# Two attention blocks on one core: row sums inverted after one transfer within SBUF, maxima 40 steps ahead instead of 32, operand splitting spread out, a new written order of the main loop

## The chip, the cores and the metric

The kernel runs on one core of a Trainium2 chip. The metric is the device time of that core in microseconds (us), the median of three runs. One further execution was recorded by the profiler; every duration below comes from that one. Engines are named as in its page: PE (TensorE, matmuls) with PEld (its weight loads), DVE (VectorE), ACT (ScalarE), POOL (GpSimd), SP (SyncE, which here only issues DMAs).

## What is computed

The inputs are two independent blocks, A and B, each with x of 1 x 2048 x 640, a wqkv of 640 x 1920 and a wo of 640 x 640, all float32, 32 heads of 20 columns. The outputs are joined on the last axis.

```
qkv = x @ wqkv
# A: each position attends to itself and to 7 earlier ones, 2 apart
idx = pos[:, None] - 2 * arange(8)[None, :]
logits = einsum("bhsd,bhswd->bhsw", q, k[idx]) * 20**-0.5     # masked where idx < 0
a = einsum("bhsw,bhswd->bhsd", softmax(logits), v[idx]) @ wo
# B: full attention over 2048 positions
b = (softmax(q @ k.T * 20**-0.5) @ v) @ wo
out = concatenate([a, b], axis=-1)
```

## The kernel before

**Operands.** Every product that needs more than the multiplier's format is made of three passes over a high and a low part (`PASSES`). A tile is loaded into a staging buffer (`stg`, three of them), cast to the high part (`first` in `parts`, by default ACT), and the low part is the subtraction raw minus high (`second`, by default DVE), L152. `split` (L157) issues the load and calls `parts` a given number of ticks later.

**Stages.** First K and Q of B are projected and stored to DRAM. Then V of B is projected in 16 groups, and between its matmuls stand the first *maxima*. After that comes the main loop of 512 steps (32 units of 4 heads x 512 queries, 16 key blocks each). One step of B is: 4 score tiles of 128 keys x 512 queries (PE), 4 exponentials of them (ACT), and 4 accumulating products with V and a column of ones (PE, `b_pv`, L436), which also gives the row sums. The maximum that is subtracted enters the scores as extra rows of q, so it must be known first: a separate pass makes the scores once more, transposed, and DVE takes their maxima (4 tiles of 128 x 512 per step, `m_reduce`, L343). That pass runs `LEAD` steps ahead: 2 x LEAD pairs of tiles are reduced between V's matmuls (L890 to L903), and as many steps at the end of the loop have no maxima.

**Order.** PE, ACT and DVE follow a written table, `ORDER` (from L946): Y is one score tile and one maxima tile, S two score tiles, M two maxima tiles that DVE reduces in one instruction, F one *token* of a projection group (two half-height matmuls side by side, 30 tokens a group), V the end of a step. The digits are PSUM banks; there are eight, one of them holds the running product with V. F groups work off the projections of A (`a_group`, L712), then A's output projection (`oa_group`) and B's (`ob_group`); groups that are left at the end run whole (`leftover`).

**POOL and SP.** POOL does A's attention (`a_scores`, `a_values`, L475 to L528). How much of it stands in each step is set by a counter that adds an assumed time per instruction (L62) and lets POOL's list run up to `STEP` us per step (L937, L938). SP issues almost every DMA from one queue in program order, so a DMA that waits for its data holds up all that stand behind it. `after(n, ...)` places an action n ticks (steps) later.

**The chain of a unit's sums.** When a unit ends, ACT copies the product out (`misc`), and `normalize` (L413) does the following: four rows of sums go to DRAM (`s_d<-misc`) and back as 128 x 16 (`sm<-s_d`), DVE inverts them, they go to DRAM (`s_d<-sm`) and return spread over the rows (`misc<-s_d`), POOL multiplies (`misc<-misc`), and the result is stored (`ot_b<-misc`). Its ticks are 1, 2, 7, 8, 9, 11 and 12 after the unit.

**The chain of maxima.** After the last tile of a unit `max_rows` (L299) transposes on DVE, casts and subtracts on POOL, and stores four pieces three ticks later (`mdr<-mtr`). They are read into the rows of q (`last<-mdr`, `s_maxima`) 9 ticks after the scores of the unit before have begun.

Of the kernel before, what the change touches and what calls it, by code (L numbers as in the profile page):

```python
# [41 lines left out]
LEAD = 32  # L42
# [3 lines left out]
STEP = 2.8  # L46
# [5 lines left out]
class InOrder:  # L52
# [5 lines left out]
    def __getattr__(self, name):  # L58
        op = getattr(self.engine, name)

        def emit(*a, **k):
            if name.startswith("tensor_"):  # L62
                n = math.prod(a[0].shape[1:])
                self.us += 0.2 + n * (0.00081 if name == "tensor_copy" else 0.0017 if len(a[0].shape) == 4 else 0.00212)
            return self.tc.keep_in_program_order(op(*a, **k))  # L65
        return emit
# [3 lines left out]
def attention_pair(ctx, tc, xa, wqk_a, wv_a, wo_a, xb, wqk_b, wv_b, wo_b, oa, ob):  # L70
# [86 lines left out]
    def split(hi, lo, src, wait, first=None, second=None, tag=("stg", 3)):  # L157
# [5 lines left out]
        sp.dma_start(raw, src)  # L163
        after(wait, parts, hi, lo, raw if len(hi.shape) == len(raw.shape) else t[:, :n], first, second,
              int(tag[0] == "stg"))
# [21 lines left out]
    def wide_pieces(src, W, half, wait, first=None, second=None):  # L187
        def piece(a, b):
# [3 lines left out]
            split(w[0][:, a:b], w[1][:, a:b], src[half][:, a:b], wait, first, second)  # L192
# [106 lines left out]
    def max_rows(u, m4):  # L299
# [14 lines left out]
        after(3, store)  # L314
# [47 lines left out]
    def s_half():  # L362
# [50 lines left out]
    def normalize(raw, u, then):  # L413
# [3 lines left out]
        s_d = dr.tile([2, GH, 512], F32, tag="s_d", bufs=4, name="s_d")  # L417

        def bcast():
            for j in range(GH):  # L420
                sp.dma_start(misc[32 * j:32 * j + 32, 512:], s_d[1, j].partition_broadcast(32))
# [8 lines left out]
        after(t[2], dve.reciprocal, sm, sm)  # L430
        after(t[3], sp.dma_start, s_d[1].rearrange("j (p c) -> j p c", c=16), sm)
        after(t[4], bcast)
        after(t[5], gp.tensor_tensor, raw, raw, misc[:, 512:], ALU.mult)
        after(t[6], then or out)
# [96 lines left out]
    def a_attention():  # L531
# [5 lines left out]
        for n, (t, c) in enumerate(UNITS):  # L537
            while any(a_rows[u[1] >= 4] <= u[0] for u in UNITS[n:n + 3]) or c == 4 and len(done_a) > 1:
                yield False
            a_fetch(n + 2)  # L540
# [4 lines left out]
            if c == 4:  # L545
                run_jobs(soft_jobs, 1)
                for _ in soft.pop(t):
                    run_jobs(soft_jobs, 1)
            if c < 4:
                yield from a_scores(t, c, a_kv.pop(n))  # L550
# [3 lines left out]
            else:  # L554
                yield from a_values(t, c - 4, a_kv.pop(n))
                if c == WIN - 1:
                    done_a.append([1, t, a_t.pop(t)[2]])
# [6 lines left out]
    def a_turn(t, o):  # L564
# [12 lines left out]
        for k in range(KC):  # L577
            job(turn_jobs, 1 + k, part, k)

    def a_back():  # L580
# [76 lines left out]
    def set_pieces(si, wait):  # L657
# [6 lines left out]
        def split_piece(b, raw):  # L664
# [3 lines left out]
            parts(AW[si][0][:, :, c:c + n], AW[si][1][:, :, c:c + n], raw, second=gp if si < 6 else dve, end=1)  # L668
            if b == len(bits) - 1:
                set_in.add(si)  # L670
# [22 lines left out]
    def xa_pieces(n):  # L693
        def piece(k):
# [3 lines left out]
            after(3, split_piece, k, raw)  # L698
# [13 lines left out]
    def a_group(si, n, a, ns):  # L712
        assert si in set_in and n in x_in, (si, n)
        if n % 2 == 0 and a == 0:
            if si + 1 < NA:
                spaced(set_pieces(si + 1, 3), 1, 2)
            else:
                spaced(wide_pieces(wo_a, WO, 0, 3, dve.tensor_copy), 1, 2)
# [15 lines left out]
    def a_done():  # L734
# [3 lines left out]
        spaced(wide_pieces(wo_a, WO, 1, 3, dve.tensor_copy), 1, 2)  # L738
# [3 lines left out]
    def oa_group(p, half, ns):  # L742
        assert ready_a[0] >= 2 * p + 2, (p, ready_a)
# [41 lines left out]
    def ob_group(qc, a, half, ns):  # L785
        assert ob_ready[0] > qc, (qc, ob_ready)
# [131 lines left out]
    def begin(i):  # L918
# [28 lines left out]
        "Y10Y32M5S47S10M2V4Y75Y61S02Y37Y56VS10Y72Y36VY51Y20Y76VY35Y21F07FFFFY36FFY52FFFY13FFY56FFFY21VM5S32VY31Y56V"  # L947
        "Y23Y51FFFFFY62FFY35FFFY16FFY23FFFM5Y21VY03S72M5VY01Y73S25VS60Y17Y32VM5S70S21VM5S37S02VM5S13Y70VY21Y65F37FFFF"
        "Y20FFY16FFFY52FFM0FFFM5VVY20Y51FFFY46FFY02FFY15FFY64FFFY02FFFF16FFY45FY30FFY72FFY54FFY30FFS72FFFM4V3VY07Y24F"
        "FFFFY05FFY72FFFY40FFY57FFFS24VS05Y71Y62VY40Y51Y27VY46Y05Y12VY74Y06Y51VY72Y40Y56VM0Y27Y45VS62M0S47VY65Y42S01V"  # L950
        "S76S54Y20VY71S60VS54M1Y76VY50Y41F27FFFFY65FFY40FFFY16FFM4FFFM0VVY64Y05FFY31FFFY46FFY50FFY13FFFY46FFFF51FFY30"
        "FY42FFY67FFY03FFY24FFFFFM6M2V0VVY64FY27FFFFY36FFY24FFFY37FFY62FFFM3VY67Y52F13FFFFY46FFY75FFFY24FFY76FFFS52V"
        "S47M5FFFFFFY42FFFFY57FY46FFFFY25VY74Y61S35VY27Y46Y13VY52Y47Y16VY35Y24Y17VY63M4S21VY76Y23S14VS57Y62Y31VY45Y27"
        "Y61VY43Y25F76FFFFY14FFY32FFFY15FFFM3FFM1VVY35Y41FFFY20FFY35FFY41FFY20FFFY35FFFY42M0S37Y65V4Y23Y70Y16VS52Y73"
        "Y01VY56Y32Y17VY05S63M1VY07F56FY31FFFY20FFY73FFFY21FFY70FFFM2VY71Y20FFFFY37FFY12FFFY30FFY17FFFM2FVS01M6Y25V"
        "Y30M6S12VY53Y01Y26VY57M0S32VY56Y73S20VS15Y67Y23VY01Y57Y63VY02F15Y76FFFFY03FFY27FFFY60FFM2FFFM6VVY20Y63FFY74F"
        "FY02FFFY63FFY47FFFY02FFFF64FFY37FY10FY52FFFY37FFY01FFY52FFFY73V0VY51Y27FFFFFY35FFY12FFFY37FFY51FFFM2VM6Y15"
        "Y42VS31M6S45VY32Y14Y76VY53F21Y47FFFFY65FFY43FFFY67FFFM3FFM5VVY37Y54FFFFFY63FFY75FFFY64FFY37FFFM5VM3S72Y15V"
# [161 lines left out]
```

## Time and profile before

| what | us |
|---|---|
| median of three runs (lowest, highest) | 1766.27 (1761.41, 1768.66) |
| the profiled execution's own time | 1765.94 |
| its span, first to last instruction | 1764.0 |
| PE, DVE, ACT, POOL busy | 1716.7, 1394.8, 1239.4, 957.2 |
| mean granted clock of PE | 0.989 |

A busy time is the time in which an engine had an instruction under way. PE's matmuls overlap and their ends are modelled, so its 97% doesn't mean that it could take no more. The stages can be told apart by what runs: K and Q of B until 147 us, V of B with the first maxima until 234, the main loop with maxima until 1642, the 32 steps without maxima until 1716, and the end.

### The profile page before, as it was taken

The page shows a single profiled execution, that of the slowest core. Times are in us where ns is not written, and L with a number is a line of the kernel's source. Part 1 is how long each engine was busy: PE and PEld are TensorE (multiplying, and loading weights), DVE is VectorE, ACT ScalarE, POOL GpSimd, SP SyncE. Part 2 cuts the span into 40 slices and gives each one's busy share as a digit, 9 for nine tenths or more (in the row PEclk, how much of TensorE's full clock was granted, in tenths as well). Part 3 has the DMA queues.
Part 4 walks back from the last instruction along what each step waited for, and adds up shares of the span by engine and source line. Part 5 has one row for each costly group of instructions (what it writes and reads, how often), then busy time and mean ns, then how long its engine had stood idle before and what let it go on. Part 6 is the DMA issues. An engine that isn't in the chain of part 4 may idle for free.

```text
span 1764.0 us, 37708 instructions
## 1 busy us (share of the span) xinstructions
PE 1716.7 (97%) x14273; PEld 1028.8 (58%) x14273; DVE 1394.8 (79%) x2083; ACT 1239.4 (70%) x2415; POOL 957.2 (54%) x857
## 2 busy tenths in 40 slices
PE   9999999999999999989999999999999999999999
PEld 7889955656655655545565555435565444443569
DVE  4326988899888888879899989988789999889101
ACT  4221278787788787777877777677777878877981
POOL 0000210100196469898899999799998994011420
PEclk9999999999999999999999999999999999999999
DMA  7675532214453365546665776367765673121222
GB/s 254 217 237 177 167 92 59 72 51 113 143 163 107 97 203 177 157 160 180 192 188 164 202 202 184 117 163 198 189 180 162 179 200 83 47 89 55 77 67 79
DMA packets 206982, 257.70 MB, mean 146 GB/s; under 512 B 98344, under 2 KB 132532, under 8 KB 205808
## 3 DMA queue, kind: packets, MB, share of 16 engines
q1 hardware_dynamic: 206164, 254.55, 49.1%
q8 instruction: 112, 1.84, 0.5%
q10 hardware_dynamic: 636, 0.74, 0.1%
q14 instruction: 70, 0.57, 0.1%
HBM read 190.31 MB, written 64.24 MB: 144 GB/s over the span
## 4 chain that ended last, share of the span: by engine, by line
PE 81%; DVE 9%; DMA 3%; POOL 3%; ACT 2%; issue 2%; SPq 1%; DVEq 0%; POOLq 0%; ACTq 0%
PE ps_st L65 81%; DVE mx L65 7%; DVE w L65 2%; POOL akv L65 2%; ACT big L65 1%; ACT last L65 1%; SPq L65 1%; DMA s_d<-sm 0%; DMA last<-qb_d 0%; POOL ao L65 0%; DMA stg<-xa 0%; DMA last<-xb 0%; DMA stg<-wo_a 0%; DMA ot_b<-misc 0%; POOL misc L65 0%
## 5 line engine op out<-in xcount | busy, mean ns | idle before, releaser
L65 DVE TENSOR_REDUCE mx<-ps_st 128x1 f32<-128x512 f32 (+1 forms) x1750 | 1255.1, 773 | 144.3 <-PE ps_st L65 136.3
L65 ACT ACTIVATE big<-ps_st 128x512 f32<-128x512 f32 x1172 | 636.4, 619 | 162.5 <-PE ps_st L65 149.2
L65 PE MATMUL ps_st<-big,last 60*128 60x512 f32 x2048 | 694.6, 434 | 10.9 <-DVE mx L65 9.9
L65 PE MATMUL ps_st<-last,big 62*128 62x512 f32 x2048 | 671.8, 427 | 28.3 <-DVE mx L65 15.5
L65 ACT ACTIVATE last<-ps_st 128x512 f32<-128x512 f32 x876 | 475.1, 619 | 117.6 <-PE ps_st L65 108.4
L65 PEld LDWEIGHTS ps_st<-last,big 62*128 62x128 f32 x2048 | 315.8, 186 | 396.1 <-DVE mx L65 121.9
L65 PE MATMUL ps_st<-w,big 64*128 64x320 f32 (+1 forms) x4560 | 491.7, 308 | 2.3 <-DVE mx L65 2.3
L65 PEld LDWEIGHTS ps_st<-w,big 64*128 64x128 f32 (+1 forms) x4560 | 432.4, 187 | 33.0 <-DVE mx L65 5.3
L65 PE MATMUL ps_st<-big,vb 128*32 128x512 f32 x2344 | 387.2, 609 | 0.0
L65 PEld LDWEIGHTS ps_st<-big,last 60*128 60x128 f32 x2048 | 311.2, 185 | 96.7 <-DVE mx L65 46.6
L65 PE MATMUL ps_st<-last,vb 128*32 128x512 f32 x1752 | 311.6, 611 | 0.1
L65 POOL TENSOR_TENSOR akv<-akv 128x640 f32<-128x640 f32 (+3 forms) x304 | 283.9, 934 | 21.4
L65 POOL TENSOR_TENSOR akv<-akv,aq 128x1280 f32<-128x1280 f32 x64 | 189.2, 2957 | 18.6 <-DMA akv<-ka_d 18.6
L65 POOL TENSOR_TENSOR akv<-akv,al 128x1280 f32<-128x1280 f32 x64 | 152.1, 2377 | 1.8 <-DMA akv<-va_d 1.7
L65 PEld LDWEIGHTS ps_st<-big,vb 128*32 128x32 f32 x2344 | 62.6, 108 | 101.3 <-issue 96.6
L65 POOL TENSOR_TENSOR misc<-misc 128x512 f32<-128x512 f32 x31 | 39.8, 1284 | 137.0 <-DMA misc<-s_d 68.4
L65 PE MATMUL ps_st<-w,last 64*128 64x320 f32 (+1 forms) x900 | 103.6, 308 | 0.0
L65 POOL CAST mtr<-mxt 128x32 fp32r<-128x32 f32 x32 | 6.7, 210 | 170.5 <-DVE mxt L65 170.5
L65 POOL TENSOR_TENSOR big<-last,big 128x1024 fp32r<-128x1024 f32 x4 | 9.5, 2406 | 155.1 <-ACT big L65 155.1
L65 PEld LDWEIGHTS ps_st<-last,vb 128*32 128x32 f32 x1752 | 48.7, 109 | 73.3 <-issue 69.9
L65 DVE TENSOR_TENSOR last<-ps_st,last 128x512 fp32r<-128x512 f32 x40 | 27.4, 690 | 77.5 <-ACT last L65 75.5
L65 PEld LDWEIGHTS ps_st<-w,last 64*128 64x128 f32 (+1 forms) x900 | 85.9, 187 | 3.5
(69 smaller groups left out, 879.3 us busy)
## 6 DMA issues: line engine op xcount, KB each, us to landing
akv<-ka_d SPq DMA_DIRECT2D x128, 320.0 KB
akv<-va_d SPq DMA_DIRECT2D x128, 320.0 KB
last<-qb_d SPq DMA_DIRECT2D x128, 160.0 KB
kb_d<-last SPq DMA_DIRECT2D x20, 512.0 KB
qb_d<-last SPq DMA_DIRECT2D x20, 512.0 KB
big<-kb_d SPq DMA_DIRECT2D x16, 640.0 KB
last<-qb_d SPq DMA_DIRECT2D x128, 80.0 KB
misc<-s_d SPq DMA_DIRECT2D x124, 64.0 KB
```

What stands on the lines that cost most here:

```text
L65: return self.tc.keep_in_program_order(op(*a, **k))
```

## The change

- `LEAD` is 40: 16 more pairs of maxima stand between V's matmuls (three per half group instead of two in every second group), and 40 steps have none. The store of the maxima is 6 ticks after the unit instead of 3, their load 5 ticks after the scores of the unit before have begun instead of 9.
- `normalize` moves the sums from SBUF to SBUF in one DMA (`sm<-misc`) instead of two through DRAM. Its ticks are 1, 5, 6, 10, 12, 14: POOL's product and the store of it are two ticks apart instead of one.
- New `parts_apart`: the cast on ACT, then the subtraction on DVE in two halves, one and two ticks later. It is used for the weights of A's second half and for wo_a, whose casts were on DVE. wo_b's casts move from DVE to ACT and its subtractions to POOL. Loads of the weights of A's projections and of wo_a are 3 ticks apart instead of 2, and these and xa are given 4 ticks to land instead of 3.
- The casts of A's transposed rows (`a_back`) move from POOL to ACT.
- POOL's list: 0.08 us more is assumed for each instruction, and `STEP` is 2.72 instead of 2.8. The loads for the next piece of A stand behind the first instruction of a piece instead of ahead of it. The transposes of A's rows on DVE come two ticks later.
- `ORDER` is a new table. It holds 2070 F tokens instead of 2100, so one more group runs whole at the end. In the first 128 steps it has 705 F tokens instead of 600.

```diff
-LEAD = 32
+LEAD = 40
-STEP = 2.8
+STEP = 2.72
-                self.us += 0.2 + n * (0.00081 if name == "tensor_copy" else 0.0017 if len(a[0].shape) == 4 else 0.00212)
+                self.us += 0.28 + n * (0.00081 if name == "tensor_copy" else 0.0017 if len(a[0].shape) == 4 else 0.00212)
+    def parts_apart(hi, lo, raw, then=None):
+        act.copy(hi, raw)
+        n = hi.shape[1] if len(hi.shape) == 3 else 1
+        step = -(-n // 2)
+        for d, a in enumerate(range(0, n, step)):
+            b = min(a + step, n)
+            after(1 + d, dve.tensor_tensor, *(t[:, a:b] if n > 1 else t for t in (lo, raw, hi.bitcast(F32))), ALU.subtract)
+
+        def end():
+            live[0] -= 1
+            if then:
+                then()
+        after(2, end)
...
-        after(3, store)
+        after(6, store)
...
-                after(9, s_maxima, u + 1)
+                after(5, s_maxima, u + 1)
...
-        t = (1, 2, 5, 6, 7, 9, 10) if then else (1, 2, 7, 8, 9, 11, 12)
-        after(t[0], sp.dma_start, s_d[0], raw[DH:128:32])
-        after(t[1], sp.dma_start, sm, s_d[0].rearrange("j (p c) -> j p c", c=16))
...
+        t = (1, 4, 5, 8, 10, 11) if then else (1, 5, 6, 10, 12, 14)
+        after(t[0], sp.dma_start, sm, raw[DH:128:32].rearrange("j (p c) -> j p c", c=16))
...
-            a_fetch(n + 2)
...
+            next(work)
+            yield
+            a_fetch(n + 2)
+            yield from work
...
-            job(turn_jobs, 1 + k, part, k)
+            job(turn_jobs, 3 + k, part, k)
...
-            parts(ot[:, 0], ot[:, 1], r, gp.tensor_copy, gp, 1)
+            parts(ot[:, 0], ot[:, 1], r, second=gp, end=1)
...
-            after(3, split_piece, k, raw)
+            after(4, split_piece, k, raw)
...
-                spaced(wide_pieces(wo_a, WO, 0, 3, dve.tensor_copy), 1, 2)
+                spaced(wide_pieces(wo_a, WO, 0, 4, apart=True), 1, 3)
...
-                spaced(wide_pieces(wo_b, WO, 0, 3, dve.tensor_copy) + wide_pieces(wo_b, WO, 1, 3, dve.tensor_copy), 1, 2)
+                spaced(wide_pieces(wo_b, WO, 0, 3, second=gp) + wide_pieces(wo_b, WO, 1, 3, second=gp), 1, 2)
...
-                    if k in (0, 8):
+                    if k in ((0, 5, 10) if o else (0, 8)):
...
-        "Y10Y32M5S47S10M2V4Y75Y61S02Y37Y56VS10Y72Y36VY51Y20Y76VY35Y21F07FFFFY36FFY52FFFY13FFY56FFFY21VM5S32VY31Y56V"
+        "Y01Y23M4S67S01M2V6Y47Y05S12M3Y07VY51F23Y40FFFFY75FFY14FFFY07FFY15FFFY04VY71Y50FFFFFY47FFY15FFFY40FFY71FFFM4V"
```

Where it moves instructions, at three places. First PE while V of B is projected: two matmuls `ps_st<-big,last` are a pair of maxima tiles, `ps_st<-w,...` are V's half matmuls, 30 of them to a half group. Before:

```order
L65 MATMUL ps_st<-big,last 128x512 x2
L65 MATMUL ps_st<-w,big 128x320 x16
L65 MATMUL ps_st<-big,last 128x512 x2
L65 MATMUL ps_st<-w,big 128x320 x8
L65 MATMUL ps_st<-w,last 128x320 x6
```

Now, in every second group of the stage:

```order
L65 MATMUL ps_st<-big,last 128x512 x2
L65 MATMUL ps_st<-w,big 128x320 x10
L65 MATMUL ps_st<-big,last 128x512 x2
L65 MATMUL ps_st<-w,big 128x320 x10
L65 MATMUL ps_st<-big,last 128x512 x2
L65 MATMUL ps_st<-w,big 128x320 x4
L65 MATMUL ps_st<-w,last 128x320 x6
```

Three pairs stand where two stood; the other groups keep two.

Second SP's queue, near the middle of the loop, while columns of A's x are loaded (`stg<-xa`). `misc<-s_d` brings the inverted sums, POOL's product `misc<-misc` follows it, and `ot_b<-misc` stores the product. Before:

```order
L65 DMA s_d<-sm 128x16
L65 DMA last<-mdr 2x1024 x2
L65 DMA misc<-s_d 32x512 x4
L65 DMA akv<-va_d 128x640 x2
L65 DMA stg<-xa 128x512
L65 DMA tr_d<-stg 128x640
L65 DMA va_d<-ro 128x320 x2
L65 DMA ot_b<-misc 20x512 x4
L65 DMA vb<-vb_d 128x4x95
L65 DMA stg<-xa 128x512
```

Now, at the same kind of place:

```order
L65 DMA misc<-s_d 32x512 x4
L65 DMA mdr<-mtr 16x2x32 x4
L65 DMA akv<-va_d 128x640 x2
L65 DMA stg<-xa 128x512 x2
L65 DMA ot_b<-misc 20x512 x4
L65 DMA va_d<-ro 128x320 x2
L65 DMA stg<-xa 128x512
L65 DMA akv<-va_d 128x640 x2
```

Two loads of xa stand ahead of the store now, which itself comes a tick later after the product; one still stands behind it. The pair `s_d<-misc`, `sm<-s_d` of the next unit has become one `sm<-misc`.

Third DVE's list in the second half of A's projections, where a weight of 128 x 5 x 128 is split (`w<-stg,w` is the subtraction, `mx<-ps_st` a reduction of maxima, with a buffer number of the unit; `stg<-ao` are transposes of A's rows). Before:

```order
L65 TENSOR_REDUCE mx_9148<-ps_st 128x1 x3
L65 TENSOR_TENSOR w<-stg,w 128x5x128
L65 STREAM_TRANSPOSE stg<-ao 128x128
L65 TENSOR_REDUCE mx_9148<-ps_st 128x1
L65 TENSOR_REDUCE mx_9148<-ps_st 128x2
L65 TENSOR_REDUCE mx_9148<-ps_st 128x1 x3
L65 TENSOR_TENSOR w<-stg,w 128x5x128
L65 TENSOR_REDUCE mx_9148<-ps_st 128x1 x5
```

Now:

```order
L65 TENSOR_REDUCE mx_8646<-ps_st 128x1 x9
L65 TENSOR_TENSOR w<-stg,w 128x3x128
L65 RECIPROCAL am<-am 128x32
L65 TENSOR_REDUCE mx_8646<-ps_st 128x1 x6
L65 TENSOR_REDUCE mx_8646<-ps_st 128x2
L65 TENSOR_TENSOR w<-stg,w 128x2x128
```

The subtraction has become two, with a step's reductions between them, and both stand a tick or two behind the cast on ACT instead of beside it.

More of the change, by code (lines that the diff above doesn't have):

```diff
@@ L155, in parts, with split @@
         (second or dve).tensor_tensor(lo, raw, hi.bitcast(F32), ALU.subtract)
-    def split(hi, lo, src, wait, first=None, second=None, tag=("stg", 3)):
+    def parts_apart(hi, lo, raw, then=None):
[10 more added lines that the diff above has]
+        after(2, end)
+    def split(hi, lo, src, wait, first=None, second=None, tag=("stg", 3), apart=False):
         t = stg(*tag)
@@ L163, in split @@
         sp.dma_start(raw, src)
+        if apart:
+            after(wait, parts_apart, hi, lo, raw)
+            return
         after(wait, parts, hi, lo, raw if len(hi.shape) == len(raw.shape) else t[:, :n], first, second,
@@ L185, in m_piece, with wide_pieces @@
         split(w[:, 0], w[:, 1], wqk_b[m], wait)
-    def wide_pieces(src, W, half, wait, first=None, second=None):
+    w_in = set()
+    def wide_pieces(src, W, half, wait, first=None, second=None, apart=False):
         def piece(a, b):
@@ L191, in piece @@
             w = W[half]
-            split(w[0][:, a:b], w[1][:, a:b], src[half][:, a:b], wait, first, second)
+            split(w[0][:, a:b], w[1][:, a:b], src[half][:, a:b], wait, first, second, apart=apart)
+            if b == KC:
+                after(wait + 2 * apart, w_in.add, id(w[0]))
         return [staged(lambda a=a, b=b: piece(a, b)) for a, b in ((0, 2), (2, 4), (4, 5))]
@@ L426, in out @@
                 sp.dma_start(ot_b[r0:r0 + DH, c0:c0 + 512], raw[32 * j:32 * j + DH])
-        t = (1, 2, 5, 6, 7, 9, 10) if then else (1, 2, 7, 8, 9, 11, 12)
-        after(t[0], sp.dma_start, s_d[0], raw[DH:128:32])
-        after(t[1], sp.dma_start, sm, s_d[0].rearrange("j (p c) -> j p c", c=16))
[L430 to L434, printed above, removed]
+        t = (1, 4, 5, 8, 10, 11) if then else (1, 5, 6, 10, 12, 14)
+        after(t[0], sp.dma_start, sm, raw[DH:128:32].rearrange("j (p c) -> j p c", c=16))
+        after(t[1], dve.reciprocal, sm, sm)
+        after(t[2], sp.dma_start, s_d.rearrange("j (p c) -> j p c", c=16), sm)
+        after(t[3], bcast)
+        after(t[4], gp.tensor_tensor, raw, raw, misc[:, 512:], ALU.mult)
+        after(t[5], then or out)
     def b_pv(i, ns):
@@ L553, in a_attention @@
                     next(soft[t])
[L554 to L557, printed above, removed]
+            elif c == WIN - 1:
+                done_a.append([1, t, a_t.pop(t)[2]])
             yield True
@@ L667, in split_piece @@
                 AW[si] = [wtile((KC, 320)) for _ in range(2)]
-            parts(AW[si][0][:, :, c:c + n], AW[si][1][:, :, c:c + n], raw, second=gp if si < 6 else dve, end=1)
-            if b == len(bits) - 1:
-                set_in.add(si)
+            hi, lo = (AW[si][x][:, :, c:c + n] for x in range(2))
+            then = (lambda: set_in.add(si)) if b == len(bits) - 1 else None
+            if si < 6:
+                parts(hi, lo, raw, second=gp, end=1)
+                if then:
+                    then()
+            else:
+                parts_apart(hi, lo, raw, then)
         bits = a_bits(si % 6)
@@ L737, in a_done @@
             aot.extend(side[:, 1280 * n:1280 * n + 1280].rearrange("p (x k c) -> p x k c", x=2, k=KC) for n in range(3))
-        spaced(wide_pieces(wo_a, WO, 1, 3, dve.tensor_copy), 1, 2)
+        spaced(wide_pieces(wo_a, WO, 1, 4, apart=True), 1, 3)
     WO = [None, None]
     def oa_group(p, half, ns):
-        assert ready_a[0] >= 2 * p + 2, (p, ready_a)
+        assert ready_a[0] >= 2 * p + 2 and id(WO[half][0]) in w_in, (p, ready_a)
         yield from f_tokens(lambda w, xi, k: aot[(2 * p + w) % 6][:, xi, k], lambda wi, k: WO[half][wi][:, k], 320, ns)
```

167 lines of the change are left out of this document (83 added, 84 removed).

## The prediction

> **What bounds the kernel now.** I read the busy time by stage first. The rows give length, then busy time (and instructions) of PE, PEld, DVE, ACT and POOL, then PE's granted clock.
>
> ```profile
> core 0: us, PE busy (x) PEld busy (x) DVE busy (x) ACT busy (x) POOL busy (x), PEclk, DMA share, GB/s
> 0.00:147.00 147.00, 144.58 (x643) 118.67 (x645) 52.68 (x78) 46.35 (x78) 3.61 (x16) 1.00 0.69 230
> 147.00:234.00 87.00, 86.16 (x1080) 83.64 (x1077) 79.74 (x71) 20.31 (x45) 16.85 (x13) 1.00 0.54 159
> 234.00:1642.00 1408.00, 1367.19 (x11522) 736.80 (x11524) 1255.18 (x1927) 1099.09 (x2139) 909.39 (x799) 0.99 0.50 142
> 1642.00:1716.00 74.00, 74.00 (x742) 45.62 (x733) 0.51 (x2) 65.94 (x138) 27.37 (x30) 1.00 0.27 79
> 1716.00:1764.00 48.00, 44.79 (x302) 44.04 (x300) 6.71 (x7) 7.69 (x18) 0.00 (x0) 1.00 0.21 76
> ```
>
> PE is busy nearly everywhere, but its matmuls overlap, so that says little. In the loop with maxima (480 of the 512 steps, 1408 us) the engine that is nearest to full is DVE: 1255.2 us, 89%, with 152.8 us idle. In the 32 steps without maxima DVE rests, and ACT is at 65.9 of 74 us. While V of B is projected both PE (86.2 of 87) and DVE (79.7) are nearly full. So I split DVE's stage by its work and its idle time. First the work, by shape, in 234 to 1642 us, and at the end one row of the whole run, the same subtraction in the first stage, where POOL is nearly idle:
>
> ```profile
> L65 DVE TENSOR_REDUCE mx<-ps_st 128x1 f32<-128x512 f32 x1450 | 909.3, 682 | 100.4 <-PE ps_st L65 95.4
> L65 DVE TENSOR_REDUCE mx<-ps_st 128x2 f32<-128x1024 f32 x234 | 282.6, 1218 | 36.9 <-PE ps_st L65 35.2
> L65 DVE TENSOR_TENSOR w<-stg,w 128x640 fp32r<-128x640 f32 x20 | 27.5, 1378 | 5.0 <-ACT w L65 4.6
> L65 DVE TENSOR_TENSOR w<-stg,w 128x320 fp32r<-128x320 f32 x10 | 8.8, 877 | 2.2 <-ACT w L65 1.8 <-DMA last<-qb_d 0.3
> L65 DVE CAST w<-stg 128x640 fp32r<-128x640 f32 x8 | 5.3, 669 | 0.8 <-DMA stg<-wo_a 0.8
> L65 DVE CAST w<-stg 128x320 fp32r<-128x320 f32 x4 | 2.4, 593 | 0.0
> ...
> L65 DVE TENSOR_TENSOR akv<-stg,akv 128x640 fp32r<-128x640 f32 x4 | 3.3, 826 | 0.0
> ```
>
> Nearly all of the work is maxima, 1191.9 us, and it can't be made less. Then the idle time of DVE in that stretch (us in total, times, longest):
>
> ```profile
> DVE mx L65 <- PE ps_st L65: 130.7, 212, 4.9
> DVE w L65 <- ACT w L65: 6.4, 8, 2.0
> DVE stg L65 <- POOL ao L65: 5.3, 1, 5.3
> DVE w L65 <- DMA stg<-wo_a: 0.8, 1, 0.8
> ```
>
> Most of it is many short waits for PE, 0.6 us each: PE, ACT and DVE hand eight banks round, and each is now and then late. The few long ones have causes further back. The timeline at 684 us shows one (SP, POOL, ACT and PE in turn), and the one at 1231 us the other kind:
>
> ```profile
> 678.87 0.80 SPq L65 DMA_DIRECT2D va_d<-ro  x2
> 685.74 1.42 SPq L65 DMA_DIRECT2D ot_b<-misc  x4
> 687.20 0.39 SPq L65 DMA_DIRECT2D vb<-vb_d  x1
> 687.63 0.50 SPq L65 DMA_DIRECT2D stg<-xa  x1
> ...
> 684.42 1.29 POOL L65 TENSOR_TENSOR misc<-misc 128x512 f32<-128x512 f32 x1
> ...
> 692.55 0.62 ACT L65 CAST big<-stg 128x512 fp32r<-128x512 f32 x1 [3.24 <-DMA stg<-xa]
> ...
> 693.72 0.50 PE L65 MATMUL ps_st<-last,big 62*128 62x512 f32 x1 [3.08 <-ACT last L65]
> ...
> 1233.16 0.29 SPq L65 DMA_DIRECT2D last<-mdr  x1
> ...
> 1237.44 0.29 PEld L65 LDWEIGHTS ps_st<-last,big 62*128 62x128 f32 x1 [4.80 <-issue]
> ```
>
> At 679.7 us SP has issued all that it may and stands before the store of a unit's product, which POOL, behind its other work, makes only at 684.4. The load of xa behind that store leaves at 687.6; ACT's cast waits 3.2 us for it, the exponentials wait behind the cast, and PE for the exponentials, 3.1 us. At 1233.2 the second half of a unit's maxima is loaded at the last moment, and PE waits 4.8 us. After such pauses the granted clock falls. Of 36 equal stretches of the span (columns as in the first view) these are all in which it is below full:
>
> ```profile
> 686.00:735.00 49.00, 43.01 (x362) 22.88 (x360) 41.56 (x63) 35.42 (x70) 45.28 (x38) 0.97 0.58 175
> 784.00:833.00 49.00, 45.27 (x388) 27.26 (x390) 44.72 (x70) 31.54 (x61) 45.52 (x40) 0.93 0.59 168
> 1078.00:1127.00 49.00, 45.47 (x386) 26.64 (x384) 44.81 (x66) 31.19 (x59) 42.04 (x34) 0.97 0.57 173
> 1127.00:1176.00 49.00, 43.53 (x284) 16.26 (x284) 44.10 (x66) 34.69 (x69) 42.68 (x40) 0.93 0.55 144
> 1225.00:1274.00 49.00, 44.44 (x376) 25.38 (x374) 38.68 (x62) 35.94 (x71) 47.27 (x41) 0.93 0.77 202
> 1568.00:1617.00 49.00, 45.46 (x256) 15.61 (x252) 45.08 (x64) 33.77 (x64) 9.59 (x11) 0.90 0.21 61
> ```
>
> The missing shares make 0.37 x 49 = 18.1 us. PE's own pauses in the stage are 1408 - 1367.2 = 40.8 us.
>
> **Term 1, the first maxima: +7 us.** 16 more pairs stand in the stage of 87 us. On DVE a pair is 282.6 / 234 = 1.21 us, together 19.3 us. DVE has 7.3 us idle there, so if every pair finds DVE full the stage grows by 12.0. At the other end PE alone sets it: 1080 matmuls in 86.2 us are 0.080 us each, 32 more are 2.6 us. Groups with two pairs remain PE's, those with three become DVE's; I take the middle, 7, to be 94.
>
> **Term 2, DVE's work in the loop: -30 us.** The same 19.3 us leave it. The casts of wo go to ACT: 5.3 + 2.4 = 7.7. The subtractions of wo_b go to POOL: 4 x 1.378 + 2 x 0.877 = 7.3. Halving the other subtractions adds 22 instructions. Two of 320 take 2 x 0.877 - 1.378 = 0.38 us more than one of 640, so 22 cost at most 8.3 us; the columns stay the same, so it isn't below 0. I take the middle, 4. Together 1255.2 - 34.3 + 4 = 1224.9.
>
> Here a rule of the Trainium skill speaks against the change. The page "SBUF — State Buffer", section "SBUF: two separate sides", says that VectorE instructions with two SBUF inputs and GpSimd instructions that read SBUF share a pair of ports as an exclusive lock: whoever starts first holds it for the whole instruction, and the other is blocked. The trace agrees in kind, 0.826 us beside an idle POOL and 1.378 beside a busy one. By the rule each of 22 further starts meets the lock anew, at 0.55 us each, 12 us instead of 4, and the forecast would be 8 us later.
>
> **Term 3, DVE's idle time in the loop: -24 us.** The long waits named above are what the edits reach: 3.1 us behind the late xa (its store now stands two ticks behind POOL's product, so SP isn't held), 4.9 behind the maxima (read four ticks earlier, and 8 steps further ahead), 5.3 behind POOL's rows (transposed two ticks later), 6.4 + 0.8 behind casts and wo (the subtraction now stands a tick behind its cast, and wo has a tick more to land): 20.5 us. Of the 18.1 us of clock I count 4, since most of that time DVE, not PE, has work to do. If no edit reaches its wait it is 0; all of PE's pauses and all of the clock would be 58.9; more idle time than before is the third rival. So 128.8 of the 152.8 us remain, and the stage becomes 1353.7.
>
> ACT gets 16 casts of A's rows and 12 of wo.
>
> ```profile
> L65 ACT CAST w<-stg 128x640 fp32r<-128x640 f32 x30 | 22.2, 752 | 0.0
> L65 POOL CAST big<-stg 128x640 fp32r<-128x640 f32 x16 | 11.5, 720 | 8.8 <-DMA stg<-tr_d 8.8
> ```
>
> At 0.75 us at most that is 21 us, and 32 exponentials leave for the next stage; ACT's 1099 us stay below DVE's 1225, so I count nothing; if DVE didn't hide it, it would be those 21. The casts of A's rows wait for the load `stg<-tr_d`; POOL waited for it once, 8.8 us. On ACT exponentials stand behind that wait, and PE behind them: 0 to 8.8, and 0 taken, since 15 of 16 found their rows there. SP loses 31 DMAs; nothing waits for their issue, 0. A's loads leave one instruction later; they are asked for nearly a whole piece ahead, 0.
>
> **Term 4, steps without maxima: +18 us.** 40 instead of 32. A step there is 74 / 32 = 2.31 us with its share of projections. ACT's 65.9 us over 32 steps are 2.06 and would be the least. 8 x 2.06 to 8 x 2.31 is 16.5 to 18.5; 18, to be 92.
>
> **Term 5, the end: +4.4 us.** One more group runs whole. Half a group takes 2.20 us there, from start to start:
>
> ```profile
> 1736.43 1.92 PE L65 MATMUL ps_st<-w,big 128*128 128x320 f32 x12
> ...
> 1738.63 1.92 PE L65 MATMUL ps_st<-w,big 128*128 128x320 f32 x12
> ```
>
> PE has no pause before the last products, so both halves count. In the loop their place goes to nobody, since DVE sets it.
>
> **The sum.** 147 + 94 + 1353.7 + 92 + 52.4 = 1739.1, and 1765.94 - 1764.0 = 1.9 outside the span: **1741 us**, against 1765.9 for the same execution, which is 0.3 us from the median of the three runs (1766.3).
>
> **The rivals.** *The waits only change place* (chance 0.20). Then the 152.8 us stay and the time is 1741 + 24 = 1765. For it: 212 of the waits are short and come from handing round the banks, which a new table does in the same manner; and the new table has 105 more F tokens in its first 128 steps. A token in the end stage is 2.20 / 15 = 0.147 us of PE, so 15.4 us more of PE's time stand where it has none to spare. Against it: the long waits have named causes, and each has an edit.
>
> *More goes than the named waits* (0.20). PE's pauses and the clock come back whole: 1741 - (58.9 - 24) = 1706; half of that rest makes 1724. For it speaks how POOL stands:
>
> ```profile
> 784.00:1470.00 686.00, 661.43 (x5582) 361.51 (x5582) 622.36 (x974) 520.17 (x1013) 634.53 (x540) 0.98 0.63 177
> POOL w L65 <- ACT w L65: 72.5, 10, 26.1
> ```
>
> From 784 to 1470 POOL is busy 92%, more than DVE's 91%, with 540 instructions whose gaps aren't counted. Its list was filled to 2.8 us a step without gaps; now gaps are counted, 0.08 us, and it is filled to 2.72, so it may stop holding up what waits for it.
>
> *POOL becomes the bound by waiting for ACT* (0.12), the slower side. Its list now holds 16 subtractions whose casts, 0.72 us each, it made itself, and which ACT now makes in its own order between exponentials. POOL's instructions stand behind such a wait, then A's rows, DVE's transposes and SP's stores. The only waits of this kind in the trace are 7.25 us each (72.5 / 10). POOL has 686 - 634.5 = 51.5 us idle in that stretch and is spared 11.5, so it decides from 63 / 16 = 3.9 us a wait; at 7.25 it adds 53: 1794. Against it: those 10 waits fell where POOL had time, and ACT is busy only 520 of 686 us there.
>
> **How the numbers follow.** The forecast, 1726 to 1757, has 0.48. A difference below 0.5%, about 9 us, can't be told from none here (the three runs lie 7 us apart). Faster by more, below 1757, are the forecast and the second case: 0.68, and 0.02 of the first case's lower end: 0.70. Within 0.5%: 0.18. Slower, above 1775: 0.12. The range reaches from the end of the second case, 1706, into the upper part of the first, 1772; the slower case and the ends of these two, together 0.18, are left out. The unknown prices lie inside it: term 1 from -4 to +5, term 2 from -2 to +8 with the lock, the idle time from -35 to +24 with the load of A's rows.
>
> **What would show it.** Right: the stage with V is near 94 us with DVE full; steps without maxima begin near 1595 us and last 92; DVE's waits for PE have none above 3 us, and the clock is 1.00 nearly throughout; no load stands for microseconds behind `ot_b<-misc` on SP; half subtractions are below 0.85 us. Wrong: DVE's idle time in the loop above 145 us, with short waits grown (the first rival); waits of POOL for ACT of over 4 us after 700 us (the third); a clock below full in as many stretches as before.

## The result, and the profile after

The changed kernel takes 1752.2 us (median of five runs, 1749.3 to 1755.4) against 1766.3 (1761.4 to 1770.7): a ratio of 0.9925, interval 0.9898 to 0.9953. It is faster by 14 us, and 11 us slower than forecast. The profiled execution took 1752.17 us, with a span of 1750.4 and a mean clock of 0.997.

Busy time by stage of the changed kernel (columns as in the prediction's first view: length, PE, PEld, DVE, ACT, POOL, clock). The loop with maxima is split at its 128th step:

```profile
core 0: us, PE busy (x) PEld busy (x) DVE busy (x) ACT busy (x) POOL busy (x), PEclk, DMA share, GB/s
...
147.00:240.00 93.00, 92.49 (x1115) 86.42 (x1115) 92.62 (x87) 20.45 (x45) 16.88 (x13) 1.00 0.52 154
240.00:637.50 397.50, 388.42 (x3507) 232.62 (x3506) 334.61 (x501) 308.69 (x597) 129.39 (x129) 0.99 0.38 105
637.50:1613.70 976.20, 960.80 (x7907) 505.33 (x7906) 896.70 (x1393) 792.09 (x1545) 765.04 (x653) 1.00 0.57 161
1613.70:1699.00 85.30, 85.29 (x762) 46.70 (x759) 0.51 (x2) 78.72 (x163) 34.33 (x37) 1.00 0.28 79
1699.00:1750.40 51.40, 47.97 (x324) 47.22 (x322) 6.71 (x7) 8.09 (x19) 0.00 (x0) 0.99 0.21 74
```

The same two parts of the loop in the kernel before:

```profile
234.00:603.80 369.80, 369.68 (x3296) 212.35 (x3295) 323.59 (x487) 300.62 (x585) 103.01 (x106) 1.00 0.34 97
603.80:1641.90 1038.10, 997.42 (x8229) 524.35 (x8232) 931.58 (x1441) 798.37 (x1554) 806.36 (x693) 0.98 0.55 158
```

Only the second part became shorter, by 61.9 us (it has 8 steps fewer, which now stand in the stage without maxima, and DVE is idle 79.5 instead of 106.5 us in it). The first 128 steps became 27.7 us longer: PE is busy 18.7 us more, DVE 11.0 more, and DVE is idle 62.9 instead of 46.2 us. Taken over the whole loop, DVE's work fell from 1255.2 to 1231.3 us, its idle time from 152.7 to 142.4.

DVE's waits in the loop of the changed kernel (us in total, times, longest):

```profile
DVE mx L65 <- PE ps_st L65: 133.4, 207, 5.7
DVE w L65 <- ACT w L65: 1.5, 1, 1.5
```

The waits for POOL's rows and for wo are gone, and of those for casts 1.5 us are left (6.4 before). Those for PE are as long in total as before (130.7). The longest of them is new. The timeline at 479 us shows POOL's product, SP's store of it, ACT's copy of the next unit's product, and DVE:

```profile
478.79 1.26 POOL L65 TENSOR_TENSOR misc<-misc 128x512 f32<-128x512 f32 x1
...
480.08 1.43 SPq L65 DMA_DIRECT2D ot_b<-misc  x4
...
482.81 0.58 ACT L65 COPY misc<-ps_st 128x512 f32<-128x512 f32 x1 [7.74 <-DMA ot_b<-misc]
...
484.32 0.69 DVE L65 TENSOR_REDUCE mx<-ps_st 128x1 f32<-128x512 f32 x1 [5.65 <-PE ps_st L65]
```

`misc` is one buffer. The store now stands 14 ticks behind a unit's end, POOL was late with the product, and 16 steps after the last copy ACT needs the buffer again: it stands for 7.7 us, with exponentials behind it, then PE, then DVE. SP too is still held by POOL's products, if for less time. The first line is the kernel before (whole run), the second the changed one (230 to 1630 us):

```profile
SPq L65 <- POOL misc L65: 82.1, 22, 10.7
```

```profile
SPq L65 <- POOL misc L65: 65.0, 17, 8.7
```

Of 36 equal stretches two in the loop are left in which the clock is below full, the first around that pause (the last stretch, in which the run ends, has 0.96):

```profile
441.00:490.00 49.00, 42.95 (x356) 25.33 (x358) 35.32 (x53) 33.62 (x65) 29.93 (x27) 0.93 0.65 178
1078.00:1127.00 49.00, 47.73 (x333) 21.04 (x332) 46.56 (x71) 39.42 (x77) 43.88 (x40) 0.97 0.51 139
```

They make 0.10 x 49 = 4.9 us of lost clock, against 18.1 before.

DVE's staged subtractions in the changed kernel (busy us, mean ns):

```profile
L65 DVE TENSOR_TENSOR w<-stg,w 128x384 fp32r<-128x384 f32 x12 | 12.2, 1013 | 1.5 <-ACT w L65 1.5
L65 DVE TENSOR_TENSOR w<-stg,w 128x256 fp32r<-128x256 f32 x12 | 10.8, 902 | 0.0
L65 DVE TENSOR_TENSOR w<-stg,w 128x320 fp32r<-128x320 f32 x10 | 9.4, 935 | 0.0
L65 DVE TENSOR_TENSOR w<-stg,w 128x128 fp32r<-128x128 f32 x6 | 8.7, 1446 | 0.0
L65 DVE TENSOR_TENSOR w<-stg,w 128x192 fp32r<-128x192 f32 x6 | 5.5, 913 | 0.0
```

Together 46.6 us, where the kernel before had 36.3 with wo_b's. A half of 128 columns takes 1.45 us on average, more than a whole of 640 did before (1.38): the length of these instructions isn't set by their columns. (An instruction's record can overlap the next one by a few hundredths of a microsecond, so sums of rows lie somewhat above the busy time of a stage.)

### The profile page after: what moved, and what is told of

Read it like the earlier page. It is cut to its first block, busy times and chain, and to the rows that moved or that the text cites. A ratio compares the mean times of both kernels' runs of the same rounds, so it can differ in the third digit from the quotient of the medians.

```text
span 1750.4 us, 37604 instructions
## 1 busy us (share of the span) xinstructions
PE 1719.3 (98%) x14243; PEld 1036.6 (59%) x14243; DVE 1383.9 (79%) x2065; ACT 1254.5 (72%) x2443; POOL 949.3 (54%) x847
## 5 line engine op out<-in xcount | busy, mean ns | idle before, releaser
L65 ACT ACTIVATE last<-ps_st 128x512 f32<-128x512 f32 x876 | 480.0, 634 | 114.9 <-PE ps_st L65 105.3
L65 PE MATMUL ps_st<-last,vb 128*32 128x512 f32 x1752 | 307.8, 604 | 0.0
L65 POOL TENSOR_TENSOR w<-stg,w 128x640 fp32r<-128x640 f32 (+1 forms) x24 | 31.7, 1327 | 174.3 <-ACT w L65 145.2
L65 POOL TENSOR_TENSOR big<-stg,big 128x512 fp32r<-128x512 f32 (+1 forms) x40 | 55.6, 1393 | 67.9 <-ACT big L65 60.8
L65 ACT COPY ro<-ps_st 128x320 f32<-128x320 f32 x154 | 59.5, 444 | 42.0 <-PE ps_st L65 27.6
```

## The experiments

Each kernel was timed in five rounds against the kernel before; ratios are to that one. Parts of the change are undone or made alone, first the table against everything else.

**The new table alone** (`order_only`).

```diff
 (kernel before)
-LEAD = 32
+LEAD = 40
-                    if k in (0, 8):
+                    if k in ((0, 5, 10) if o else (0, 8)):
-    ORDER = (...)
+    ORDER = (...)
```

The table is that of the changed kernel, which needs LEAD of 40 and the third pair.

> The kernel before with LEAD of 40, the third pair in two of four groups and the new table; all other code as before. My theory (the other edits reach the waits and DVE's work; the table by itself only moves things between stages): the stage with V 6 us longer, 19.3 us of maxima out of the loop, the steps without maxima 11 us and the end 3.4 us longer, so +1.4 us from stages; in the first 128 steps 17 us more of DVE's idle time as in the changed kernel, and the long waits stay: 1766 to 1785 us. Rival (the table is what saved the time, since it was fitted to these waits): 1752 us within 5.

1783.2 us, ratio 1.0107 (1.0087 to 1.0127): 17 us slower, as my theory had it. Its first 128 steps:

```profile
239.70:633.80 394.10, 389.00 (x3511) 232.69 (x3513) 329.25 (x498) 309.56 (x598) 132.10 (x131) 0.99 0.38 109
```

They are 24.3 us longer than before with none of the other edits, PE 19.3 us busier. So the loss in the first quarter comes with the table: its 105 more F tokens stand where PE was busy for 369.7 of 369.8 us already. Here the store of the sums has its old tick, 12, and in the same place, at 478.7 us, ACT still waits 5.1 us for it: a part of the pause of the changed kernel came with the table as well.

**The other edits on the old table** (`edits_only`).

```diff
 (changed kernel)
-LEAD = 40
+LEAD = 32
-STEP = 2.72
+STEP = 2.8
-                self.us += 0.28 + n * (...)
+                self.us += 0.2 + n * (...)
-        after(6, store)
+        after(3, store)
-                after(5, s_maxima, u + 1)
+                after(9, s_maxima, u + 1)
-                    if k in ((0, 5, 10) if o else (0, 8)):
+                    if k in (0, 8):
 (and the table of before)
```

> The changed kernel with the old table, LEAD of 32, the old pace of GpSimd and the old times of the maxima's transfers; the new transfer for the sums with its later ticks, casts and subtractions apart and halved, A's casts on ACT, wo's edits, the later transposes and loads of A stay. My theory: DVE's work in the loop falls by 7.7 for wo's casts and 7.3 for wo_b's subtractions and grows by the halving, 4 to 17; the waits for xa, for POOL's rows and for casts go, 15 us; the wait for maxima (4.9 us) stays: 1740 to 1757 us. Rival (the edits serve only the new table): 1766 us within 5.

1761.6 us, ratio 0.9984 (0.9966 to 1.0002): 5 us, which can't be told from none, and less than my theory wanted. The wait for maxima, which was to stay with LEAD of 32 and the old times, isn't in the trace: no wait of PE above 3 us is left but one of 5.1 us behind ACT's copy, at 510.9 us, where ACT waits for the store. The two halves of the change, +17 and -5, don't add up to -14. Either the pace and the maxima's times, which neither half had, carry the rest, or the parts work together. The new pace with the old table wasn't tried: A's rows would there come after the group that reads them.

**Whole subtractions** (`whole`).

```diff
 (changed kernel, parts_apart)
-        step = -(-n // 2)
+        step = n
```

> The changed kernel with each staged subtraction as one instruction of all its columns, one step after the cast, in place of two halves one and two steps after it. Theory of the lock (each further start beside GpSimd meets it anew): DVE's staged subtractions fall from 46.6 us in the loop to about 29, and the time by the 12 to 17 us that the halves cost more, to 1735 to 1740, if DVE's work sets the loop one to one. Rival (DVE is idle 142 us in that stage, so that a saved us there is lost to waiting for PE): 1748 to 1754. Second rival (a long subtraction holds up the maxima behind it, and PE): 1755 or more.

1742.4 us, ratio 0.9866 (0.9844 to 0.9888): 10 us faster than the changed kernel, between my theory and its rival. DVE's staged subtractions there:

```profile
L65 DVE TENSOR_TENSOR w<-stg,w 128x640 fp32r<-128x640 f32 x16 | 18.4, 1152 | 1.5 <-ACT w L65 1.5
L65 DVE TENSOR_TENSOR w<-stg,w 128x320 fp32r<-128x320 f32 x8 | 7.5, 936 | 0.0
```

25.9 us instead of 46.6: each of the 22 starts that are spared was worth 20.7 / 22 = 0.94 us of DVE, and half of that shows in the time. Why a start costs so much can be read in the changed kernel. POOL starts an instruction at 603.87, DVE a half subtraction 0.13 us later:

```profile
603.87 2.92 POOL L65 TENSOR_TENSOR akv<-akv,aq 128x1280 f32<-128x1280 f32 x1
604.00 3.20 DVE L65 TENSOR_TENSOR w<-stg,w 128x384 fp32r<-128x384 f32 x1
...
742.36 0.55 DVE L65 TENSOR_TENSOR w<-stg,w 128x384 fp32r<-128x384 f32 x1
```

The half ends at 607.20, which is 0.41 us after POOL's instruction (603.87 + 2.92). With POOL idle, at 742.36, the same shape takes 0.55. The Trainium skill ("SBUF — State Buffer", section "SBUF: two separate sides") calls this an exclusive lock that whoever starts first holds for its whole instruction. The trace agrees instruction by instruction: of the twelve halves of 384 columns three ran with POOL idle and two began in the last 0.11 us of an instruction of POOL, and these five took 0.54 to 0.56 us; the other seven all ended 0.41 to 0.42 us after the instruction that POOL had begun before them, however long that still ran, and took 0.62 to 3.20. The mean price of a further start was above the 0.55 us that the prediction put beside that rule.

**The store two ticks earlier** (`store12`).

```diff
 (changed kernel, normalize)
-        t = (1, 4, 5, 8, 10, 11) if then else (1, 5, 6, 10, 12, 14)
+        t = (1, 4, 5, 8, 10, 11) if then else (1, 4, 5, 8, 10, 12)
```

> The changed kernel with the product and the store of a unit's sums two steps earlier, at steps 10 and 12 behind the unit's end instead of 12 and 14, with the sums' way there one step shorter at three places. My theory (in the changed kernel ACT's copy of the next unit waits 7.7 us for that store at 475 us, and PE 5.8): the pause goes, 1744 to 1748. Rival (the store then stands before SP while POOL is late, as in the kernel before, and holds up the loads behind it): the pause moves to a load, 1752 us or more, with a load that stands behind the store for microseconds.

The product and its way there move with the store, so the two ticks between product and store stay.

1748.7 us, ratio 0.9905 (0.9887 to 0.9923), just above the range of my theory. The interval overlaps that of the changed kernel, so the 3.5 us can't be told from none. In the trace ACT's wait for the store (8.4 us in 2 times) is gone. The rival shows faintly: SP stands 76.5 us before POOL's product in place of 65.0, and ACT waits for a load of wv_a once for 3.4 us in place of 1.7.

**Both** (`whole_12`): the edits of the last two.

> The changed kernel with both of the last two edits: each staged subtraction whole, and a unit's product and store two steps earlier. My theory: the two causes are apart (DVE held behind GpSimd's instructions; ACT's copy held behind the store), so their gains of 10 and 3.5 us add up: 1737 to 1741 us. Rival (both only give DVE time in the same steps): 1742 to 1746 us.

1734.4 us, ratio 0.9815 (0.9802 to 0.9828). On whole subtractions the earlier store brings 8 us, clear of both intervals, more than on halves. With `w12_norm_old` below this is the fastest kernel of the study: 32 us below before, 18 below the change. Its loop in the same two parts:

```profile
239.60:628.10 388.50, 384.95 (x3511) 229.65 (x3510) 331.42 (x498) 308.76 (x597) 129.58 (x129) 1.00 0.39 107
628.10:1593.50 965.40, 955.50 (x7906) 503.62 (x7906) 884.34 (x1374) 791.23 (x1545) 766.54 (x653) 1.00 0.57 163
```

Against the changed kernel the first part is 9.0 us shorter, where the pause at 479 us was, the second 10.8, where DVE has 12.4 us less work.

**The old pace** (`pace`).

```diff
 (changed kernel)
-STEP = 2.72
+STEP = 2.8
-                self.us += 0.28 + n * (...)
+                self.us += 0.2 + n * (...)
```

> The changed kernel with the old pace of GpSimd's list: 2.8 us a step, with 0.2 in place of 0.28 us for each instruction. The old table with the other edits gained 5 us, the new table alone lost 17, together they gained 14, so some 26 us come from what neither had, the pace or the maxima's transfers, or from their working together. Theory of the pace: GpSimd's list, filled beyond what it does in a step, falls behind, and with it the rows, transposes and products that wait for it: 1758 to 1775 us, with DVE's idle time from the 128th step on above 90 us, against 74 now. Rival (GpSimd's lateness is hidden): 1749 to 1756 us.

1768.3 us, ratio 1.0008 (0.9995 to 1.0020): the whole gain is lost with two constants. From the 128th step to the last maxima (635.2 to 1628.1 us) DVE is idle 92.5 us, against 79.5 in the changed kernel counted in the same way (the 74 in the expectation fits a count that stops at 1603 us). So 13 of the 16 us are idle time of DVE, as the theory had it, and one reason is more definite than "falls behind". ACT's waits for the store, in 230 to 1630 us, of the changed kernel and then of this one:

```profile
ACT misc L65 <- DMA ot_b<-misc: 8.4, 2, 7.7
```

```profile
ACT misc L65 <- DMA ot_b<-misc: 22.6, 6, 7.7
```

One of the six, near 1382 us (POOL, SP, ACT, DVE):

```profile
1381.79 1.26 POOL L65 TENSOR_TENSOR misc<-misc 128x512 f32<-128x512 f32 x1
...
1383.08 1.43 SPq L65 DMA_DIRECT2D ot_b<-misc  x4
...
1385.80 0.58 ACT L65 COPY misc<-ps_st 128x512 f32<-128x512 f32 x1 [6.33 <-DMA ot_b<-misc]
...
1387.30 0.69 DVE L65 TENSOR_REDUCE mx<-ps_st 128x1 f32<-128x512 f32 x1 [4.92 <-PE ps_st L65]
```

SP stands 91.8 us before POOL's products here, 65.0 in the changed kernel. A list that is filled too far delays one product, and the store at tick 14 has nothing left to give. The rest of the 16 us is spread over stretches of a microsecond or so and isn't named here.

**The old times of the maxima** (`maxold`).

```diff
 (changed kernel)
-        after(6, store)
+        after(3, store)
-                after(5, s_maxima, u + 1)
+                after(9, s_maxima, u + 1)
```

> The changed kernel with the old times of the maxima's transfers: stored three steps after the last pair in place of six, read nine steps after a unit's start in place of five. Theory (LEAD of 40 alone gives the maxima 8 steps, so reading them earlier brings nothing): 1749 to 1756 us. Rival (the maxima are still read at the last moment, or their store stands before SP while GpSimd is late): PE waits for them as before, 4.9 us or several times that, 1757 to 1775 us.

1757.0 us, ratio 0.9938 (0.9925 to 0.9951), not told apart from the changed kernel. The number stands at the edge between theory and rival, but PE's wait at the last moment for maxima (4.8 us before) doesn't come back in the trace, so the new times aren't what removes it. LEAD of 40 isn't needed for it either, since `edits_only` has neither and is without that wait. Which edit takes it away isn't shown.

**Cast and subtraction in one step** (`together`).

```diff
 (changed kernel, parts_apart's body)
+        parts(hi, lo, raw, end=1)
+        if then:
+            then()
-                after(wait + 2 * apart, w_in.add, id(w[0]))
+                after(wait, w_in.add, id(w[0]))
```

> The changed kernel with each staged subtraction whole and in the same step as its cast, as before the change. Theory (the step between them is what took DVE's waits for casts away): against the kernel with whole subtractions a step later, 1742.4 us, DVE waits for ACT again, 6 to 11 us, in 8 to 11 waits: 1747 to 1753 us. Rival (the waits only take idle time that DVE has anyway): 1740 to 1745 us.

1762.4 us, ratio 0.9981 (0.9968 to 0.9994): cast on ACT and whole subtraction on DVE are both issued at once here, and it is 20 us slower than `whole`, from which it differs only by the tick between them, and more than any of my cases. DVE's staged subtractions and the waits in front of them (third column):

```profile
L65 DVE TENSOR_TENSOR w<-stg,w 128x640 fp32r<-128x640 f32 x16 | 23.7, 1483 | 8.2 <-ACT w L65 8.2
L65 DVE TENSOR_TENSOR w<-stg,w 128x320 fp32r<-128x320 f32 x8 | 10.5, 1312 | 3.6 <-ACT w L65 3.6
```

DVE waits 11.8 us for casts instead of 1.5, and the subtractions take 34.2 us instead of 25.9: 18.6 us, about as much as the 20; that they show in the time one to one isn't shown. The waits were expected. Why the subtractions themselves meet more of POOL's instructions there was not settled.

**The old way of the sums** (`w12_norm_old`): `whole_12` with the `normalize` of before, through DRAM, with its ticks 1, 2, 7, 8, 9, 11, 12.

```diff
 (whole_12, normalize)
-        after(t[0], sp.dma_start, sm, raw[DH:128:32].rearrange("j (p c) -> j p c", c=16))
+        after(t[0], sp.dma_start, s_d[0], raw[DH:128:32])
+        after(t[1], sp.dma_start, sm, s_d[0].rearrange("j (p c) -> j p c", c=16))
...
```

> The kernel with whole subtractions and the earlier store (1734.4 us), with the old way of the sums: out to DRAM by one transfer more, and back, the reciprocal at step 7, the product at 11, the store at 12. My theory (the transfer that is spared is off the path; what counts is when the store stands before SP): 1732 to 1738 us. Rival (31 transfers fewer on SP, or the time of the product one step earlier, is a part of the gain): 1741 us or more, with the store again before SP while GpSimd is late.

1734.2 us, ratio 0.9815 (0.9802 to 0.9828), the same as `whole_12`. With the store at tick 12 the transfer that is spared, and the tick of the product, bring nothing that can be measured. It shows one thing more: SP stands 113.4 us before POOL's products, against 77.4 in `whole_12`, and another 66.3 us before `s_d<-misc`, and ACT waits 4.7 us for the store at 478 us. So the rival's condition, a store before SP while POOL is late, holds, and still the time is the same: a queue that stood longer cost nothing here, where no needed load stood behind it for long.

**The table against the table** (`table`): the changed kernel with the edits of `pace` and of `maxold` together. It differs from `edits_only` in the table, LEAD and the first pairs alone; the three go together.

> The changed kernel with the old pace and the old times of the maxima's transfers together: against the run with the old table and otherwise the same code, 1761.6 us, only the table, LEAD and the place of the first pairs differ. My theory (the table costs, mostly in its first 128 steps, and the pace and the maxima's times bring 16 and 5 us independent of each other): 1770 to 1776 us. Rival (pace and maxima's times cure the same lateness, and the table is neutral): 1758 to 1766 us.

1770.8 us, ratio 1.0024 (1.0011 to 1.0037), against 0.9984 (0.9966 to 1.0002): with everything else equal the table, with its LEAD, costs 9 us, and its first 128 steps took 394 us against 378. It is not neutral.

**A's casts on POOL again** (`w12_poolcast`).

```diff
 (whole_12, a_back)
-            parts(ot[:, 0], ot[:, 1], r, second=gp, end=1)
+            parts(ot[:, 0], ot[:, 1], r, gp.tensor_copy, gp, 1)
```

> The kernel with whole subtractions and the earlier store (1734.4 us), with the 16 casts of A's rows on GpSimd again. Theory (GpSimd limits what waits for it from the 128th step on, and 16 casts of 0.72 us are 11.5 us of its time, each also blocking DVE's subtractions): 1738 to 1748 us. Rival (GpSimd waits for ACT's casts instead, about 50 us in 8 waits, so nothing was won by moving them): 1728 to 1737 us.

1740.6 us, ratio 0.9851 (0.9837 to 0.9866): 6 us slower, so the casts are better on ACT, as the first theory said. POOL's waits for them, which the prediction feared, fall from 51.5 us in 8 times to 8.6 in 3, but they had cost less than the casts do.

**A still slower pace** (`w12_slower`): `whole_12` with `STEP = 2.68`.

> The fastest kernel so far (whole subtractions, the earlier store, 1734.4 us) with GpSimd's list filled to 2.68 us a step in place of 2.72. Theory (a list that is lighter by step holds up DVE's subtractions and SP's stores less; the step from 2.8 and 0.2 to 2.72 and 0.28 brought 16 us for some 60 us less work asked of GpSimd between steps 128 and 416, and this is 12 us less): 1730 to 1733 us. Rival (at 2.72 GpSimd keeps up already, and A's rows only come later): 1733 to 1740 us.

1753.1 us, ratio 0.9926 (0.9908 to 0.9943): 19 us slower, against the theory and beyond the rival. A lighter list isn't a better one. Near 1370 us POOL's subtraction of A's rows comes late, and PE has a group before it that reads them (PE's and DVE's waits shown in brackets):

```profile
1370.37 1.53 POOL L65 TENSOR_TENSOR big<-stg,big 128x640 fp32r<-128x640 f32 x1
...
1371.96 0.90 PE L65 MATMUL ps_st<-w,big 64*128 64x320 f32 x3 [4.38 <-POOL big L65]
...
1373.74 0.69 DVE L65 TENSOR_REDUCE mx<-ps_st 128x1 f32<-128x512 f32 x1 [7.92 <-PE ps_st L65]
```

That is the rival's mechanism, 7.9 us. The subtractions on DVE happen to meet more of POOL's instructions, 34.7 us instead of 27.7, and near 465 us ACT's cast waits 4.3 us for a load of wv_a, after which DVE is idle 5.1 us where it was idle 3.7. So the pace is bound on both sides, by A's rows and by the sums' product, and it seems to decide by chance what DVE's subtractions meet. The two sides were tried on different kernels; 2.8 us a step with the earlier store wasn't tried.

## Why the prediction was right and wrong

The direction was right, with the range and the order of size of each stage; 11 us were missing. By its terms, from the profiled runs:

| term | forecast | measured |
|---|---|---|
| 1, first maxima (87 us stage) | +7 | +6.0 |
| 2, DVE's work in the loop | -30.3 | -23.9 |
| 3, DVE's idle time in the loop | -24 | -10.4 |
| 4, steps without maxima | +18 | +11.3 |
| 5, the end | +4.4 | +3.4 |
| sum | -24.9 | -13.6 |

*Term 1* has the right number, but not by its mechanism. DVE is full in the whole stage, 92.62 of 93 us, and not in every second group alone. It isn't 12 us because a full DVE took 92.1 us for 81 pairs, 1.14 each, where the term has 1.21. PE's end of the bracket was wrong as well: 32 more matmuls were 6.3 us of PE and not 2.6, since the mean of 0.080 us was taken over V's half matmuls too. Both engines are full now, and which of them sets the 6.0 isn't shown; that the middle hit it is luck. *Term 5* came as reckoned.

*Term 4* has 85.3 us instead of 92, below what it called the least. It priced 8 more steps at the old share of projections. The new table has 150 F tokens in its last 40 steps, where the old one had 180 in 32, and PE has 762 matmuls there against 742. The 30 tokens that go to the end are gone from here; I had said that their place goes to nobody. At 0.147 us they are 4.4 us of the 6.7. This helped.

*Term 2 failed in one sum: the halving.* I took 4 us, the middle between 0 and the price of columns, though row and rule both spoke for more. Forecast for the staged subtractions was a fall of 3.3 us in the loop (7.3 of wo_b less, 4 for the halves more); the rows went from 36.3 to 46.6, up by 10.3. The highest price that I allowed, 8.3 us, was too low too: `whole` puts it at 20.7 us of DVE and 10 us of time, where the rule had 12 and the forecast 4. "Half subtractions are below 0.85 us" was wrong too: their means are 0.90 to 1.45. wo's casts and subtractions left DVE as reckoned, and the maxima fell by 21.7 us in the rows instead of 19.3, so the term as a whole missed by less.

*Term 3 failed in what I set at nothing, and in one premise.* The longest wait for PE is 5.7 us where I wanted none above 3, and the 142 us of idle time lie just under the 145 that I had set as the mark of the first rival. The named long waits did go (the late xa, the maxima, POOL's rows, most of the casts, wo), and 13 of the 18 us of clock in the loop came back, where I had counted 4. But the idle time fell by 10, not 24. The first 128 steps have 16.7 us more of it. Some 5.8 of these come with the pause at 479 us: in `whole_12`, which doesn't have it, that part has 57.1 us idle, in the changed kernel 62.9. The other 10.9 are the first rival with its 105 F tokens, which I gave 0.20 as a whole, though it holds for a quarter of the loop; `order_only` and `table` show that it comes with the table. The premise was that the store, two ticks behind POOL's product, no longer holds SP. It still does (65.0 us in 17 waits, and some 8 us ahead of the very store at 480 us); what went is the load that was needed behind it. And the later store now holds ACT's copy. I had named what stood behind the store on SP, and not who needs the buffer that it empties.

*The separation of casts and subtractions* I priced by the waits alone, 7.2 us. `together` against `whole` shows 20. *POOL's pace* I priced at nothing in the sum and mentioned under the second rival: on the changed kernel it is worth 16 us, and what that rival named shows in the traces, since at the old pace SP and ACT stand longer behind POOL's products (91.8 and 22.6 us instead of 65.0 and 8.4). That less is always better doesn't follow: on `whole_12` a still lighter list is worse (`w12_slower`). *The casts of A's rows* on ACT were set at nothing and bring 6 us on `whole_12`. *The sums' transfer within SBUF* was set at nothing, and `w12_norm_old` agrees.

So the small net result holds large parts of both signs: table +9 to +17, halving +10, late store +8 on whole subtractions (3.5 on halves, not clear of none), against separation -20, pace -16, A's casts -6. They were measured on different kernels and don't simply add. *The third rival* (POOL bound by waiting for ACT) is refuted by the time and by `w12_poolcast`, though the sign that I had set for it came: POOL waits for ACT's casts of A's rows for up to 18.1 us after 700 us, 60.8 us in 9 times over the loop. From 784 to 1470 us, where the rival was reckoned, it is

```profile
POOL big L65 <- ACT big L65: 15.3, 4, 6.2
```

and POOL has 82.0 us idle there, so the waits fall where it has time. The prediction's line of 72.5 us for such waits is one of the whole run; in that stretch the kernel before had none. What wo's edits, the later transposes and the later loads of A are worth alone wasn't tried.

## What to carry to other kernels

When an instruction is cut in pieces, price each start by what it may have to wait out, not by its columns: here 22 more starts beside a busy POOL cost 10 us. When a store is moved later to free its queue, look for who needs the buffer next, and when, and look afterwards whether the queue is free. When a wait is gone, undo the edit that was meant for it before crediting it: the wait for maxima went without LEAD and without the new times. A pace or a table that was fitted to one kernel is worth only what the rest of that kernel lets it be: try it up and down before calling it a cause.

## What the runs showed of the hardware

A subtraction of 128 x 384 with both inputs in SBUF took 0.55 us on DVE while POOL was idle and 3.20 us when POOL had begun an instruction of 2.92 us just before it. Seven of the twelve in the run ended 0.41 to 0.42 us after an instruction that POOL had begun before them. Long pauses of PE went with a lower clock: the changed kernel's one pause above 3 us, 5.5 us at 483 us, lies in a stretch of 49 us at 0.93, and `whole_12`, which has none above 3 us in the loop, has a mean clock of 0.999. The reverse doesn't hold: in the kernel before the stretch from 1568 to 1617 us is at 0.90 without such a pause. A change of 1.5% in a constant that only sets the order of POOL's list (2.72 to 2.68, on `whole_12`) moved the time by 1.1%.
